# Turning two half chunks at once, and value preparation in slots of its own

## The chip, the cores and the metric

The kernel runs on one core of a Trainium2 chip. Its engines work side by side, each through its own list of instructions in order: TensorE (PE, matmuls and transposes; PEld is its loading of stationary operands), VectorE (DVE), ScalarE (ACT), GpSimd (POOL) and SyncE (SP), which here issues the DMAs. The metric is the device time of one execution in microseconds; lower is better. Before the change the median of three runs was 1085.4 us (1083.91 to 1087.75).

## What is computed

An attention over keys and values that are averaged in groups of 8 along the sequence, followed by a gated product of matrices without an activation:

```python
B, H, S, D = 8, 8, 576, 64          # batches, heads, sequence, head size
k_p = k.reshape(B, H, 72, 8, D).mean(axis=3)
v_p = v.reshape(B, H, 72, 8, D).mean(axis=3)
scores = (q @ k_p.T) / sqrt(D)      # per batch and head, 576 x 72
attn = softmax(scores)
o = attn @ v_p                      # 576 x 64 per head
x = o over all heads, 4608 tokens x 512
out = ((x @ w_a) * (x @ w_b)) @ w_out     # w_a, w_b 512 x 1536, w_out 1536 x 512
```

All data are float32. The kernel keeps near float32 precision with matmuls in fp32r: each operand is split into a high part and a low part (`low_part`, L188, subtracts the high part from the source), and three products (high x high, high x low, low x high) are summed.

## The kernel before

**The long part.** The 4608 tokens are cut into 9 tiles of 512 (t = 0 to 8). For each tile and each of 12 slices f of the 1536 hidden columns, `ffn_in` makes 24 matmuls of 512 columns (12 into psa, L635 to L637, then 12 into psb), `gated` multiplies the two on DVE (h, L592), `split_gated` splits the product into hh and hl, and `ffn_out` adds 12 matmuls into four accumulators (L657 to L659). After a tile's last slice the accumulators are copied to y and stored through SP (L666). This is 36 matmuls per slice and tile, 3888 in all, and the order of these items is written out by hand in `order`.

**The attention in between.** The attention of a later tile is worked out between the matmuls of the tile before. Tokens are taken in chunks of 128 or 64 (`chunks_of`): a batch of 576 tokens is four chunks of 128 and one of 64, the 64 last in even batches and first in odd ones. From tile 2 on, the two neighbouring halves of 64 (the last of an even batch and the first of the next) form one *band* that goes through scores and softmax together, the first half in partitions 0 to 63 and the second in 64 to 127. There are three such bands, in tiles 3, 5 and 7.

`chunk` loads a band's queries, splits them (qh, ql), makes the scores on PE (psc, L452 and L459), sums their halves on DVE (s, L466), subtracts the maximum (L419, L420), takes the exponential on ACT (L480) and the sum and its inverse on DVE (L482 to L484), scales on POOL (L486), and splits the probabilities into pr (high and low, for 64 of the 72 pooled keys) and rem (the other 8). Then each unit of the band (one chunk of 128, or each of the two halves of 64) is handed to `turn_unit`: for x = 0, 1 four transposes each, for x = 2 two transposes (L538) into a PSUM tile ptr, followed by one ACT copy (L539) into the block's operand `turned[j][x]`. A *block* is one to three units of one batch within one tile. When its last unit is turned, the block's value products follow: matmuls po (L573 to L576) against vdiag and vrem, whose result becomes xh and xl, the input of `ffn_in`.

psc, ptr and po share one ring of two PSUM buffers with the tag "att". An instruction that writes such a buffer waits until the reader of the buffer's former content is done.

**Keys and values.** `load_values(b)` loads a batch's values in three pairs of DMAs into a ring of two buffers ("kv", shared with the keys), reduces each of the six over its groups of 8 on DVE (vp, L339), writes the high part to vdiag on ACT (L344), spreads the remainder into the temporary vwide (two instructions, L348), copies it to vrem on ACT (L359), writes vdiag's low part in two instructions on DVE (L362), and finally vrem's low part (L188). vdiag and vrem exist twice, by b % 2. vwide is from the ring "tmp" of six places, which queries, stored outputs y and others use as well.

**What sets the order.** Every engine runs its instructions in the order in which the program writes them. `Chains` decides that order: each of these pieces of work is a generator. `chains.step()` is called twice per psa or psb group and twice per `ffn_out`, that is once for each six matmuls; one call is a *slot*. `yield n` puts a generator off by n slots, `yield PE` lines it up for work on PE, of which one is let through per slot. Within a slot, generators run by rank: products, splits, chunks, weights, keys and values. The work between two yields goes to the engines without a break. `plan` starts each band's `chunk` some slots ahead of its need, `load_keys` of the next batch 18 slots (`KEYS_AHEAD`) ahead of that, and `load_values` 16 slots (`VALUES_AFTER`) behind the keys, so two slots ahead of the chunk. The slot arithmetic knows no engine's time: an instruction that is late simply delays what is written behind it on its engine.

Batches 0 and 1 are prepared at the start, beside the conversion of the weights; batch 2 falls at the end of that phase, and batches 3 to 7 into the long part.

Of the kernel before, what the change touches and what calls it, by code (L numbers as in the profile page):

```python
# [10 lines left out]
F32R = mybir.dt.float32r  # L11
# [9 lines left out]
P = 128  # L21
# [5 lines left out]
NK = DM // P  # L27
# [20 lines left out]
NG = H // 4  # L48
# [4 lines left out]
BLOCK, BLOCK_LATER = 256, 384  # L53
# [26 lines left out]
class Chains:  # L80
# [9 lines left out]
    def mark(self, *what):  # L90
        self.done.add(what)
# [30 lines left out]
def attn_moe_kernel(ctx: ExitStack, tc: tile.TileContext, q, k, v, vr, wa, wb, wo, out):  # L122
    nc = tc.nc
    const = ctx.enter_context(tc.tile_pool(name="const", bufs=1))
    sb = ctx.enter_context(tc.tile_pool(name="sb", bufs=2))
# [12 lines left out]
    ident = const.tile([P, P], F32R, name="ident")  # L138
# [16 lines left out]
    bands, i = [], 0  # L155
# [157 lines left out]
    def load_values(b):  # L313
        vd = vdiag[b % 2]
        vrem = sb.tile([P, NG, 2, 2, D], F32R, tag="vrem", name=f"vrem_{b}")
        yield from wait(("keys", b, 2), ("values", b - 1))
        vp = sb.tile([P, NK + NG, D], F32, tag="vp", name=f"vp_{b}", bufs=1)
        for x0 in range(0, NK + NG, 2):
            if b == 0:
                vraw = [early_v[:, x, :] if x < NK else early_vr[:, x - NK, :] for x in (x0, x0 + 1)]  # L320
            else:
                if x0:
                    yield from wait(("vraw", b, x0 - 2))
                vraw = [sb.tile([P, S], F32, tag="kv", name=f"vraw_{b}_{x0 + j}")[:, :D * POOL] for j in range(2)]
                for j in range(2):
                    if x0 < NK:
                        nc.sync.dma_start(vraw[j], v[b, :, x0 + j, :])
                    else:
                        nc.sync.dma_start(vraw[j][:NR], vr[b, :, x0 + j - NK, :])
                yield 3  # L330
            for j in range(2):
                x, rows = x0 + j, P if x0 < NK else NR
                vv = vraw[j][:rows].rearrange("p (d j) -> p d j", j=POOL)
                if b == 0 and 0 < x < NK:
                    for n in (4, 2, 1):
                        to = vp[:rows, x].unsqueeze(2) if n == 1 else vv[:, :, :n]
                        nc.gpsimd.tensor_tensor(out=to, in0=vv[:, :, :n], in1=vv[:, :, n:2 * n], op=ALU.add)
                else:
                    nc.vector.tensor_reduce(out=vp[:rows, x], in_=vv, axis=AX.X, op=ALU.add)  # L339
            mark("vraw", b, x0)  # L340
            yield 1
        for e in range(2):
            r = slice(e * KM, e * KM + KM)
            nc.scalar.mul(vd[r, :, 0, r], vp[r, :NK], 1.0 / POOL)  # L344

        wide = tmp(f"vwide_{b}").rearrange("p (r j e d) -> p r (j e) d", r=NG, j=2, e=2)
        for r in range(NG):
            nc.vector.scalar_tensor_tensor(  # L348
                out=wide[:NR, r],
                in0=vp[:NR, NK + r].unsqueeze(1).broadcast_to([NR, 4, D]),  # L350
                scalar=1.0 / POOL,
                in1=mask[:NR].unsqueeze(2).broadcast_to([NR, 4, D]),
                op0=ALU.mult,
                op1=ALU.mult,
            )
        wide = wide.rearrange("p r c d -> p (r c d)")
        vrf = vrem.rearrange("p r j e d -> p (r j e d)")
        yield 1
        nc.scalar.copy(vrf[:NR], wide[:NR])  # L359
        for e in range(2):  # L360
            r = slice(e * KM, e * KM + KM)
            nc.vector.scalar_tensor_tensor(  # L362
                out=vd[r, :, 1, r],
                in0=vp[r, :NK],
                scalar=1.0 / POOL,
                in1=vd[r, :, 0, r].bitcast(F32),
                op0=ALU.mult,
                op1=ALU.subtract,
            )
        yield 1  # L370
        r = slice(2 * 4 * KR, NR)
        low_part(nc.vector, vrf[r], wide[r], vrf[r])
        yield 1
        vrems[b] = vrem
        mark("values", b)

    def chunk(i):
# [121 lines left out]
        low_part(nc.gpsimd, pr[:n, 1], s[:n, :, :KM], pr[:n, 0])  # L499
        low_part(nc.gpsimd, rem[:n, :, 1], sr, rem[:n, :, 0])  # L500
        mark("probs", i)
        for u, us in units:
            yield 1 if soon else PROBS_GAP
            yield from turn_unit(u, pr[us], rem[us], ident[us, us])
        mark("turned", i)

    def turn_unit(i, pr, rem, ident):

        b, o, n = flat[i]
        t, col = divmod(b * S + o, NT)  # L510
        soon = t < 2
        j = block_of[i]
        members = blocks[j]
        c0 = sum(flat[c][2] for c in members if c < i)
        total = sum(flat[c][2] for c in members)
        if i == members[0]:
            turned[j] = {}

        def turn(x):
            rows = P if x < 2 else NR  # L520
            num = NK if x < 2 else NG
            if x not in turned[j]:
                if tile_of[i] < 2:
                    turned[j][x] = sb.tile([P, num, BLOCK], F32R, tag=f"p{x}", name=f"p{x}_{j}", bufs=1)
                elif x == 0:
                    both = sb.tile([P, 2, NK, BLOCK_LATER], F32R, tag="work", name=f"p_{j}", bufs=1)
                    turned[j].update({0: both[:, 0], 1: both[:, 1]})
                else:
                    turned[j][x] = sb.tile([P, NK * BLOCK], F32R, tag="p0", name=f"p{x}_{j}", bufs=1)[
                        :, :NG * BLOCK_LATER  # L530
                    ].rearrange("p (g s) -> p g s", g=NG)
            dst = turned[j][x]
            pt = ps.tile([P, 512], F32, tag="att", name=f"ptr_{i}_{x}", bufs=2)
            ptr = pt.bitcast(F32R).rearrange("p (g s) -> p g s", g=NK)
            for g in range(num):
                src = pr[:, x, 2 * g:2 * g + 2, :] if x < 2 else rem[:, g]
                src = src.rearrange("p a s -> p (a s)") if x < 2 else src.rearrange("p a c s -> p (a c s)")
                nc.tensor.transpose(ptr[:rows, g, :n], src, ident)  # L538
            nc.scalar.copy(dst[:rows, :, c0:c0 + n], ptr[:rows, :num, :n])  # L539

        yield from wait(("turn", i - 1), ("value", j - 1))
        if t >= 2:
            yield from wait(*(("weight", name, NF - 1) for name in ("a", "b", "o")))
        for x in range(3):
            if x < 2 or t < 2:
                yield PE
            turn(x)
            if x != 1 or t < 2:
                yield 1
        mark("turn", i)  # L550
        if i != members[-1]:
            return
        yield 1 if soon else VALUE_GAP
        yield from wait(("values", b))
        if t not in xtiles:
            xtiles[t] = [sb.tile([P, NK, NT], F32R, tag=x, name=f"{x}_{t}") for x in ("xh", "xl")]
        xh, xl = xtiles[t]
        vd, vrem = vdiag[b % 2], vrems[b]
        cols = slice(col + n - total, col + n)
        per = min(NK, 512 // total)  # L560
        th, tl, tr = (turned[j][x] for x in range(3))
        for g0 in range(0, NK, per):
            yield PE
            if j == 0:
                po = ps.tile([P, 512], F32, tag="psb" if g0 else "psa", name=f"po_{j}_{g0}")
            else:
                po = ps.tile([P, 512], F32, tag="att", name=f"po_{j}_{g0}", bufs=2)
            pov = po[:, :per * total].rearrange("p (g s) -> p g s", g=per)
            for g in range(g0, g0 + per):
                if per == NK and g == NK // 2:  # L570
                    yield PE
                dst = pov[:, g - g0, :]
                nc.tensor.matmul(dst, vd[:, g, 0, :], th[:, g, :total], start=True, stop=False)  # L573
                nc.tensor.matmul(dst, vd[:, g, 0, :], tl[:, g, :total], start=False, stop=False)
                nc.tensor.matmul(dst, vd[:, g, 1, :], th[:, g, :total], start=False, stop=False)  # L575
                nc.tensor.matmul(  # L576
                    dst,
                    vrem[:NR, g // 2, g % 2].rearrange("p e d -> p (e d)"),
                    tr[:NR, g // 2, :total],
                    start=False,  # L580
                    stop=True,
                )
            gs = slice(g0, g0 + per)
            nc.scalar.copy(xh[:, gs, cols], pov)
            yield 1
            low_part(nc.vector, xl[:, gs, cols], pov, xh[:, gs, cols])
        mark("value", j)
        del turned[j]
# [231 lines left out]
```

## Time and profile before

| | us |
|---|---|
| median of three runs | 1085.4 |
| the profiled execution, its own time | 1088.85 |
| its span, first to last instruction | 1087.1 |
| PE busy | 1035.4 (95%) |
| DVE busy | 566.6 (52%) |
| ACT busy | 510.6 (47%) |
| POOL busy | 503.3 (46%) |

The mean granted clock of PE over the span was 0.987 of full speed. A row of the timeline gives start, length (both in us), engine, line, operation, result and operands with their size, how many were merged, and in brackets how long the engine stood idle before it and who released it. A row of a stretch gives its bounds and length, the busy us of PE, PEld, DVE, ACT and POOL with counts of instructions, the granted clock of PE, the share of time that DMA engines were busy, and GB/s. A row of groups gives busy us, the mean ns of one, and the idle time before them.

### The profile page before, as it was taken

Reading aid. Unit: us, or ns where it says so; the run is one execution under the profiler, and the core shown is the slowest. Engines: PE = TensorE matmul, PEld = TensorE weight load, DVE = VectorE, ACT = ScalarE, POOL = GpSimd, SP = SyncE. Lnnn points to the kernel's source line nnn. Section 1 sums busy time; section 2 is a strip of 40 time slices with the busy share of each in tenths; the row PEclk is TensorE's granted clock in tenths of the full one; section 3 lists DMA queues with packets and bytes.
Section 4 is the critical chain, followed back from the end, with each engine's and each line's share of the span. In section 5 each row is a group of like instructions: output and inputs, shape, how many; then the busy total and the mean of one; then the engine's idle time right before and its main releaser. Section 6 shows DMA issues by size and latency. Waiting matters only on the chain.

```text
span 1087.1 us, 13530 instructions
## 1 busy us (share of the span) xinstructions
PE 1035.4 (95%) x4964; PEld 860.9 (79%) x4964; DVE 566.6 (52%) x914; ACT 510.6 (47%) x1023; POOL 503.3 (46%) x428
## 2 busy tenths in 40 slices
PE   4568999999999999999999999999999999999998
PEld 4456788788878888888878888888878888888886
DVE  7889967744672346544672337543573344322112
ACT  3656645445554445444544445444544354443332
POOL 6322200045474555555554555554554355555442
PEclk9979999999999999999999999999999999999999
DMA  6335445214220003000320003100310010001001
GB/s 219 105 120 155 147 136 170 92 54 137 77 96 1 1 23 126 27 1 1 100 85 1 1 1 109 44 1 1 121 54 2 1 59 1 1 1 39 1 1 39
DMA packets 32178, 63.79 MB, mean 59 GB/s; under 512 B 7376, under 2 KB 7376, under 8 KB 32112
## 3 DMA queue, kind: packets, MB, share of 16 engines
q1 hardware_dynamic: 32112, 62.93, 18.0%
q8 instruction: 39, 0.64, 0.2%
q14 instruction: 27, 0.22, 0.1%
HBM read 51.38 MB, written 11.53 MB: 58 GB/s over the span
## 4 chain that ended last, share of the span: by engine, by line
PE 84%; DVE 10%; ACT 3%; DMA 2%; issue 1%; POOL 0%; SPq 0%; DVEq 0%; ACTq 0%; POOLq 0%
PE psb L635 9%; PE acc L657 9%; PE psb L637 8%; PE psb L636 8%; PE psa L635 8%; PE acc L659 8%; PE acc L658 8%; PE psa L636 8%; PE psa L637 8%; PE ptr L538 2%; PE psc L452 2%; DVE vp L339 1%; DVE vwide L348 1%; PE po L575 1%; PE psc L459 1%
## 5 line engine op out<-in xcount | busy, mean ns | idle before, releaser
L592 DVE TENSOR_TENSOR h<-psb,h 128x512 f32<-128x512 f32 x108 | 74.6, 691 | 352.6 <-PE psb L637 345.5
L188 POOL TENSOR_TENSOR jlb<-wb_raw,jhb 128x512 fp32r<-128x512 f32 x88 | 115.1, 1308 | 271.4 <-ACT jhb L267 271.4
L188 POOL TENSOR_TENSOR jlo<-wo_raw,jho 128x512 fp32r<-128x512 f32 x108 | 142.9, 1323 | 116.8 <-ACT jho L267 116.8
L642 ACT COPY h<-psa 128x512 f32<-128x512 f32 x108 | 63.5, 588 | 242.3 <-PE psa L637 230.9
L635 PE MATMUL psb<-xh,jhb 128*128 128x512 f32 x432 | 173.3, 401 | 0.8 <-DVE h L592 0.8
L635 PE MATMUL psa<-xh,jha 128*128 128x512 f32 x432 | 173.2, 401 | 0.0
L657 PE MATMUL acc<-jho,hh 128*128 128x512 f32 x432 | 171.9, 398 | 0.0
L636 PE MATMUL psa<-xl,jha 128*128 128x512 f32 x432 | 169.5, 392 | 0.7 <-DVE xl L188 0.7
L637 PE MATMUL psb<-xh,jlb 128*128 128x512 f32 x432 | 169.8, 393 | 0.0
L636 PE MATMUL psb<-xl,jhb 128*128 128x512 f32 x432 | 169.7, 393 | 0.0
L637 PE MATMUL psa<-xh,jla 128*128 128x512 f32 x432 | 169.6, 393 | 0.0
L659 PE MATMUL acc<-jho,hl 128*128 128x512 f32 x432 | 168.6, 390 | 0.0
L658 PE MATMUL acc<-jlo,hh 128*128 128x512 f32 x432 | 168.3, 389 | 0.0
L188 POOL TENSOR_TENSOR jla<-wa_raw,jha 128x512 fp32r<-128x512 f32 x88 | 121.8, 1384 | 78.7 <-ACT jha L267 71.6
L605 ACT CAST hh<-h 128x512 fp32r<-128x512 f32 x100 | 62.2, 622 | 93.6 <-DVE h L592 89.6
L188 DVE TENSOR_TENSOR hl<-h,hh 128x512 fp32r<-128x512 f32 x100 | 85.5, 855 | 35.8 <-ACT hh L605 35.6
L637 PEld LDWEIGHTS psb<-xh,jlb 128*128 128x128 f32 x432 | 81.9, 190 | 17.6
L637 PEld LDWEIGHTS psa<-xh,jla 128*128 128x128 f32 x432 | 81.8, 189 | 17.5
L635 PEld LDWEIGHTS psb<-xh,jhb 128*128 128x128 f32 x432 | 82.1, 190 | 16.7 <-DVE h L592 1.2
L659 PEld LDWEIGHTS acc<-jho,hl 128*128 128x128 f32 x432 | 81.1, 188 | 17.5
L636 PEld LDWEIGHTS psa<-xl,jha 128*128 128x128 f32 x432 | 82.0, 190 | 15.8 <-DVE xl L188 1.1
L636 PEld LDWEIGHTS psb<-xl,jhb 128*128 128x128 f32 x432 | 82.2, 190 | 15.1
(95 smaller groups left out, 1678.2 us busy)
## 6 DMA issues: line engine op xcount, KB each, us to landing
out<-y SPq DMA_DIRECT2D x36, 256.0 KB, 2.1
kraw<-in_k SPq DMA_DIRECT2D x28, 288.0 KB, 3.3
qraw<-in_q SPq DMA_DIRECT2D x28, 256.0 KB, 3.6
vraw<-in_v SPq DMA_DIRECT2D x28, 256.0 KB, 2.9
words<-in_wa SPq DMA_DIRECT2D x12, 512.0 KB, 3.5
words<-in_wb SPq DMA_DIRECT2D x12, 512.0 KB, 3.5
words<-in_wo SPq DMA_DIRECT2D x12, 512.0 KB, 3.5
vraw<-in_vr SPq DMA_DIRECT2D x14, 192.0 KB, 2.8
```

The lines of the kernel that those rows point to most:

```text
L188: eng.tensor_tensor(out=lo, in0=src, in1=hi.bitcast(F32), op=ALU.subtract)
L452: nc.tensor.matmul(pt[:n, :2 * hk], qh[:, g, :n], kd[:, g].rearrange("p w e s -> p (w e s)"), start=(x == 0), stop=False,)
L538: nc.tensor.transpose(ptr[:rows, g, :n], src, ident)
L592: nc.vector.tensor_tensor(out=h, in0=pt, in1=h, op=ALU.mult)
L605: nc.scalar.copy(hh, h)
L635: nc.tensor.matmul(pt, wh[:, c], xh[:, kk], start=(kk == 0), stop=False)
L636: nc.tensor.matmul(pt, wh[:, c], xl[:, kk], start=False, stop=False)
L637: nc.tensor.matmul(pt, wl[:, c], xh[:, kk], start=False, stop=(kk == NK - 1))
L642: nc.scalar.copy(h, pt)
L657: nc.tensor.matmul(acc[c], hh[:, cs], wh, start=first, stop=False)
L658: nc.tensor.matmul(acc[c], hh[:, cs], wl, start=False, stop=False)
L659: nc.tensor.matmul(acc[c], hl[:, cs], wh, start=False, stop=last)
```

## The change

Two things are changed. In `load_values`, for batches 2 to 7, a yield is put behind each reduction, behind each vwide instruction, and two slots behind each low-part instruction of vdiag; batches 0 and 1 stay as they were. In `turn_unit`, the first half of a two-half band transposes all 128 rows at once; the first 64 columns of the result go to its own block's operand as before, and the other 64 are copied by ACT to a tile kept aside (in buffers p1 and p2, which the first two tiles used). When the second half's turn comes, it takes no PE work, and ACT copies the kept columns to its block's operand.

```diff
@@ load_values
                 else:
                     nc.vector.tensor_reduce(out=vp[:rows, x], in_=vv, axis=AX.X, op=ALU.add)
+                if b > 1:
+                    yield 1
             mark("vraw", b, x0)
             yield 1
...
             nc.vector.scalar_tensor_tensor(out=wide[:NR, r], ...)
+            if b > 1:
+                yield 1
...
             nc.vector.scalar_tensor_tensor(out=vd[r, :, 1, r], ...)
+            if b > 1:
+                yield 2
         yield 1
@@ chunk
+        halves = {}
         for u, us in units:
             yield 1 if soon else PROBS_GAP
-            yield from turn_unit(u, pr[us], rem[us], ident[us, us])
+            yield from turn_unit(u, pr[:n], rem[:n], halves, us.start > 0)
@@ turn_unit
-    def turn_unit(i, pr, rem, ident):
+    def turn_unit(i, pr, rem, halves, kept):
...
-        soon = t < 2
+        soon, full = t < 2, pr.shape[0]
...
             dst = turned[j][x]
+            if kept:
+                nc.scalar.copy(dst[:rows, :, c0:c0 + n], halves[x][:rows])
+                return
             pt = ps.tile([P, 512], F32, tag="att", name=f"ptr_{i}_{x}", bufs=2)
...
-                nc.tensor.transpose(ptr[:rows, g, :n], src, ident)
+                nc.tensor.transpose(ptr[:rows, g, :full], src, ident[:full, :full])
             nc.scalar.copy(dst[:rows, :, c0:c0 + n], ptr[:rows, :num, :n])
+            if n < full:
+                if x != 1:
+                    tag, shape = ("p2", [P, NG, BLOCK]) if x else ("p1", [P, NK, BLOCK])
+                    half = sb.tile(shape, F32R, tag=tag, name=f"half{x}_{i}", bufs=1).rearrange("p g s -> p (g s)")
+                    for y in (x,) if x else (0, 1):
+                        halves[y] = half[:, y % 2 * NK * n:][:, :(NG if y == 2 else NK) * (full - n)].rearrange(
+                            "p (g s) -> p g s", s=full - n
+                        )
+                nc.scalar.copy(halves[x][:rows], ptr[:rows, :num, n:full])
...
         for x in range(3):
-            if x < 2 or t < 2:
+            if (x < 2 or t < 2) and not kept:
                 yield PE
             turn(x)
```

## The prediction

> **What bounds the kernel now.** I read the page's first lines, then the busy time by stretches, then the rows of TensorE (PE) that began late, then what VectorE (DVE) was doing just before them.
>
> ```profile
> span 1087.1 us, 13530 instructions
> PE 1035.4 (95%) x4964; PEld 860.9 (79%) x4964; DVE 566.6 (52%) x914; ACT 510.6 (47%) x1023; POOL 503.3 (46%) x428
> ```
>
> ```profile
> 316.00:557.00 241.00, 241.00 (x1177) 201.32 (x1176) 120.86 (x190) 114.75 (x234) 130.34 (x108) 1.00 0.13 41
> 557.00:564.20 7.20, 4.79 (x18) 3.92 (x17) 6.46 (x10) 1.96 (x4) 2.44 (x3) 0.76 0.06 23
> 564.20:813.40 249.20, 249.20 (x1220) 208.43 (x1218) 121.29 (x192) 118.06 (x240) 132.44 (x110) 1.00 0.11 36
> 813.40:820.50 7.10, 4.69 (x21) 3.83 (x19) 6.09 (x10) 1.46 (x3) 1.92 (x3) 0.76 0.00 0
> ```
>
> In the stretches (length, then busy us of PE, PEld, DVE, ACT, POOL, then the granted clock) PE is busy for all of 241.0 and 249.2 us at clock 1.00. There only two things shorten the kernel: less work on PE, or the removal of the few places where PE stands. From 193 us on, PE's late rows are these five:
>
> ```profile
> 199.31 0.50 PE L635 MATMUL psb<-xh,jhb 128*128 128x512 f32 x1 [0.76 <-DVE h L592]
> 211.31 0.40 PE L452 MATMUL psc<-kdiag,qh 128*128 128x288 f32 x1 [1.69 <-DVE s L466]
> 312.88 0.40 PE L452 MATMUL psc<-kdiag,qh 128*128 128x288 f32 x1 [1.18 <-DVE s L466]
> 560.26 0.54 PE L452 MATMUL psc<-kdiag,qh 128*128 128x288 f32 x1 [2.40 <-DVE s L466]
> 816.14 0.43 PE L452 MATMUL psc<-kdiag,qh 128*128 128x288 f32 x1 [2.41 <-DVE s L466]
> ```
>
> Together 8.44 us. Four are score matmuls (L452) that need a buffer of the ring "att", which the score sum on DVE (L466) empties late. DVE was late because the value preparation stood in front of it:
>
> ```profile
> 207.91 1.28 DVE L339 TENSOR_REDUCE vp<-vraw 96x64 f32<-96x512 f32 x2 [2.58 <-DMA vraw<-in_vr]
> 310.55 1.78 DVE L188 TENSOR_TENSOR vrem<-vwide,vrem 32x512 fp32r<-32x512 f32 x1
> 435.24 0.75 DVE L348 SCALAR_TENSOR_TENSOR vwide<-vp,mask 96x256 f32<-96x256 f32 x2
> 553.83 1.23 DVE L339 TENSOR_REDUCE vp<-vraw 96x64 f32<-96x512 f32 x2
> 556.01 1.85 DVE L348 SCALAR_TENSOR_TENSOR vwide<-vp,mask 96x256 f32<-96x256 f32 x2
> 557.78 1.94 DVE L362 SCALAR_TENSOR_TENSOR vdiag<-vp,vdiag 64x256 fp32r<-64x256 f32 x2
> 559.75 0.82 DVE L466 TENSOR_REDUCE s<-psc 128x144 f32<-128x288 f32 x2
> ```
>
> Batch 5: two pairs, 1.85 and 1.94 us, run in one piece ahead of the sum at 559.75. Each stretched pair is two short instructions (batch 4's vwide pair took 0.75 us), the second of which ends with a POOL instruction beside it:
>
> ```profile
> 556.27 1.30 POOL L188 TENSOR_TENSOR pr<-s,pr 128x512 fp32r<-128x512 f32 x1 [0.73 <-ACT pr L495]
> ```
>
> Behind three of the five stalls the clock sinks:
>
> ```profile
> 211.30:215.60 4.30, 4.29 (x13) 3.48 (x14) 2.84 (x7) 0.46 (x2) 0.00 (x0) 0.61 0.00 0
> 560.20:564.20 4.00, 3.94 (x14) 3.54 (x15) 3.33 (x7) 0.00 (x0) 0.00 (x0) 0.57 0.00 0
> 816.10:820.50 4.40, 4.36 (x19) 3.83 (x19) 3.46 (x6) 0.00 (x0) 0.00 (x0) 0.61 0.00 0
> ```
>
> Work at clock c loses (1 - c) of its time: 0.39 x 4.30 + 0.43 x 4.00 + 0.39 x 4.40 = 5.1 us.
>
> **The change, first part: values in slots of their own.** A slot is six 512-column matmuls, 6 x 0.23 = 1.4 us where nothing else is put in (the spacing is quoted below). Counting yields from a batch's first reduction: before, the reductions (L339) stand at slots 0, 0, 4, 4, 8, 8, vwide at 9, 9, vdiag at 10, 10, the vrem low part at 11. After, for batches 2 to 7: reductions 0, 1, 6, 7, 12, 13, vwide 15, 16, vdiag 18 and 20, vrem 23, done at 24. The chunk planned with the same begin reaches its score sums at slots 9 to 11 (its load waits 5, its two query steps 1 and QUERY_GAP 4); in batch 3, whose chunk waits for another, at 12 and 13. So in batches 2, 4, 5, 6 and 7 nothing of the values stands at slots 9 to 11, and in batch 3 one reduction per slot (0.6 us, half of the 1.23 us pair) stands where vwide, vdiag and vrem stood before. I count the four score stalls as gone: 1.69 + 1.18 + 2.40 + 2.41 = 7.7 us. The stall at 199.31 has two reductions ahead of h (L592); one moves behind it: 0.6 of the 0.76 us. With the clock's 5.1 us: 13.4 us.
>
> [...] By the rows, each of the three stalls from 1.69 us up has its dip and no dip lies within the two long full stretches; I go by the rows.
>
> Where the moved work lands, DVE has room:
>
> ```profile
> 564.20:582.00 17.80, 17.80 (x90) 14.32 (x89) 4.46 (x8) 8.77 (x20) 10.57 (x9) 1.00 0.00 1
> ```
>
> After batch 5's old place DVE is busy 4.46 of 17.8 us. The five pieces add at most 1.85 + 1.94 + 1.78 = 5.6 us there. Without this cover they would be back in front of the sums, at the old price.
>
> What the stretch makes late is the value product. Batch 7 has the least room:
>
> ```profile
> 792.41 1.27 DVE L339 TENSOR_REDUCE vp<-vraw 128x64 f32<-128x512 f32 x2
> 816.48 0.68 DVE L188 TENSOR_TENSOR vrem<-vwide,vrem 32x512 fp32r<-32x512 f32 x1
> ```
>
> ```profile
> 857.04 0.19 PE L573 MATMUL po<-p,vdiag 128*128 128x64 f32 x1
> ```
>
> Eleven slots took 24.1 us, 2.2 each with everything put in; 12 more are 26 us against 857.04 - 817.16 = 39.9 us of room, so 13 us are left, less two slots by which the second half gets earlier: no cost.
>
> The moved steps issue DMAs: second and third pair of value loads leave 2 and 4 slots later on SP's queue. In batch 4 the second pair thereby falls behind the stores of a finished tile:
>
> ```profile
> 425.36 3.02 SPq L666 DMA_DIRECT2D out<-y  x4
> vraw<-in_v SPq DMA_DIRECT2D x28, 256.0 KB, 2.9
> ```
>
> At worst 3.0 + 2.9 us to landing against three slots (4.2 us): DVE would wait 1.7 us, with an h (L592) behind it that PE needs only some slots later. I take 0 and keep 1.7 for the range. In batch 2 it goes the other way: five slots instead of four lie between the second pair's last reduction and the use of the third, so the 2.58 us wait for the load should shrink; it is in the stall at 211.31 already. The temporary vwide is held from slot 15 to 23 instead of 9 to 11; its ring has six places and fewer than six requests fall in that time: 0.
>
> **Second part: one turn for two halves.** Three bands (tiles 3, 5, 7) hold two halves of 64. What a turn costs PE is the start of the second matmul behind it less the last start ahead of it, less two matmuls:
>
> ```profile
> 423.25 0.39 PE L637 MATMUL psb<-xh,jlb 128*128 128x512 f32 x1
> ...
> 424.08 0.39 PE L658 MATMUL acc<-jlo,hh 128*128 128x512 f32 x1
> ...
> 425.01 0.39 PE L659 MATMUL acc<-jho,hl 128*128 128x512 f32 x1
> ...
> 425.98 0.39 PE L658 MATMUL acc<-jlo,hh 128*128 128x512 f32 x1
> ```
>
> ```profile
> 574.30 0.39 PE L636 MATMUL psb<-xl,jhb 128*128 128x512 f32 x1
> 574.53 0.39 PE L637 MATMUL psb<-xh,jlb 128*128 128x512 f32 x1
> ...
> 575.62 0.39 PE L658 MATMUL acc<-jlo,hh 128*128 128x512 f32 x1
> ...
> 576.52 0.39 PE L659 MATMUL acc<-jho,hl 128*128 128x512 f32 x1
> ...
> 577.75 0.40 PE L658 MATMUL acc<-jlo,hh 128*128 128x512 f32 x1
> ```
>
> Spacing 0.23 us, so a whole chunk of ten transposes costs 0.83 + 0.97 - 4 x 0.23 = 0.88 us and a half of ten 1.09 + 1.23 - 0.92 = 1.40 us: a half is dearer than a whole. A band goes from 2.80 to 0.88 us; 3 x 1.92 = 5.8 us.
>
> It adds three copies on ACT per band:
>
> ```profile
> L539 ACT CAST p<-ptr 128x256 fp32r<-128x256 f32 x16 | 5.9, 372 | 16.1 <-PE ptr L538 16.0
> L539 ACT CAST p<-ptr 96x128 fp32r<-96x128 f32 x8 | 2.1, 265 | 0.0
> ```
>
> 2 x 0.37 + 0.27 = 1.0 us, 3.0 in all, on an engine busy 8.8 of 17.8 us in the stretch above. The first buffer of "att" is held 0.37 us longer, but its next user comes about 2 us after it (the two groups start at 574.5 and 576.5). Without that room: 3.0 us. The copies of the second half no longer wait for PE. I take 0.
>
> **Sum.** 13.4 + 5.8 = 19.2 us: span 1087.1 - 19.2 = 1067.9. The profiled execution took 1088.85, so 1069.7 by its own time. That execution is 3.45 us above the median of the three shown (1085.4): from the median 1066.2. Clock dips are what I would expect to differ between executions, and then the median had less to lose; I take the middle, 1068.0, with 1064 to 1072 as its own range.
>
> **Rivals.**
> - The stalls return in part. For: the pieces still meet POOL one by one, and batch 3 still has a reduction in each slot of its sums. Against: batch 4 carried all pieces beside its sums without a PE wait. Half of 13.4 lost: 1074.7.
> [...]
> - The values part does not do what it says, because POOL's hold, not the order, makes DVE late: 1068.0 + 13.4 = 1081.4. Against: the held pieces no longer stand before a sum.
> - Slower. Five pieces spread over 24 slots each meet a POOL instruction, and in a longer stretch some chunk's sums always stand behind a held one. Price 2.40 + 1.72 = 4.1 us per stall; it decides from 19.2 / 4.1 = 4.7 new stalls, and one per batch (six) gives 1068.0 + 24.6 = 1092.6. For: the rows with 1.85, 1.94 and 1.78 us. Against: a single piece leaves most of a slot free, and slots 9 to 11 are empty of values. [...]
>
> **Chances.** Forecast 0.62, stalls in part 0.16, dips stay 0.08, values part idle 0.08, slower 0.06. About 0.3% (3.3 us) is what a measurement here tells from no change. Of the values-part case I give 0.03 to faster, 0.05 to no change: faster 0.89, same 0.05, slower 0.06. The range 1062 to 1077 holds the first three.
>
> **What would show it.** Right: no PE row waiting for L466 behind 193 us; vwide, vdiag and vrem one by one between other DVE work; clock 1.00 through the former dips; 30 fewer transposes, none in the form 64x128 in tiles 3, 5, 7; nine more ACT copies. Wrong: a PE wait for DVE at 12 or more slots behind a batch's first reduction, PE waiting for ACT's p in the three bands, or a value product held by vrem in batch 7.

## The result

The changed kernel takes 1068.96 us (median of four runs, 1068.24 to 1069.69) against 1084.89 us of the kernel before in the same comparison. The ratio is 0.9849, 95% interval 0.9828 to 0.987: 15.9 us faster. Forecast: 1068.0 us, range 1062 to 1077. Repeated beside other runs it was 1069.58 against 1086.36, ratio 0.9843 (0.983 to 0.9857).

The first lines of the profile after, whose execution took 1068.24 us:

```profile
span 1066.5 us, 13486 instructions
PE 1023.5 (96%) x4934; PEld 854.5 (80%) x4934; DVE 575.4 (54%) x914; ACT 511.8 (48%) x1032; POOL 504.3 (47%) x428
```

PE has 30 instructions less, ACT nine more, as listed in the prediction. PE's rows that began late behind 193 us are now two instead of five:

```profile
197.08 0.50 PE L655 MATMUL psb<-xh,jhb 128*128 128x512 f32 x1 [0.17 <-DVE h L612]
306.83 0.40 PE L458 MATMUL psc<-kdiag,qh 128*128 128x288 f32 x1 [1.01 <-DVE s L472]
```

The sum of the waits fell from 8.44 to 1.18 us. The stretches (bounds and length; then busy us of PE, PEld, DVE, ACT, POOL; then the granted clock) show 744 us without a gap where before there were two gaps and two dips of the clock:

```profile
193.00:217.00 24.00, 23.83 (x109) 19.56 (x108) 19.34 (x34) 9.92 (x21) 4.01 (x4) 1.00 0.21 70
300.00:316.00 16.00, 14.99 (x80) 12.41 (x79) 12.13 (x23) 8.56 (x18) 8.85 (x8) 1.00 0.52 176
316.00:1060.00 744.00, 744.00 (x3598) 623.76 (x3597) 337.65 (x509) 338.22 (x682) 395.49 (x323) 1.00 0.09 29
```

DVE around batch 5 after the change. The two pairs of score sums (L472) come first, with nothing of the values right ahead of the second; vwide, vdiag and vrem follow:

```profile
547.87 0.94 DVE L472 TENSOR_REDUCE s<-psc 128x144 f32<-128x288 f32 x2 [0.29 <-PE psc L465]
550.24 0.94 DVE L472 TENSOR_REDUCE s<-psc 128x144 f32<-128x288 f32 x2 [1.42 <-PE psc L465]
...
552.68 0.67 DVE L339 TENSOR_REDUCE vp<-vraw 96x64 f32<-96x512 f32 x1
...
556.94 2.81 DVE L350 SCALAR_TENSOR_TENSOR vwide<-vp,mask 96x256 f32<-96x256 f32 x2
559.67 1.51 DVE L366 SCALAR_TENSOR_TENSOR vdiag<-vp,vdiag 64x256 fp32r<-64x256 f32 x1
...
563.40 1.03 DVE L366 SCALAR_TENSOR_TENSOR vdiag<-vp,vdiag 64x256 fp32r<-64x256 f32 x1
...
565.18 0.68 DVE L188 TENSOR_TENSOR vrem<-vwide,vrem 32x512 fp32r<-32x512 f32 x1
```

The pieces are no shorter: vwide takes 2.81 us where it took 1.85. Nor did the yields part them all: vwide's two instructions and the first of vdiag run back to back, from 556.94 to 561.18. They are merely where nobody on PE waits. And DVE now waits for PE ahead of the second pair of sums (1.42 us), where before PE waited for DVE.

The one turn of a two-half band in tile 5, PE in order of time:

```profile
562.18 0.39 PE L657 MATMUL psb<-xh,jlb 128*128 128x512 f32 x1
562.41 0.45 PE L549 MATMUL ptr<-ident,pr 128*128 128x128 f32 x4
562.70 0.46 PE L677 MATMUL acc<-jho,hh 128*128 128x512 f32 x1
563.00 0.40 PE L678 MATMUL acc<-jlo,hh 128*128 128x512 f32 x1
...
563.92 0.39 PE L679 MATMUL acc<-jho,hl 128*128 128x512 f32 x1
...
564.89 0.40 PE L678 MATMUL acc<-jlo,hh 128*128 128x512 f32 x1
```

By the prediction's rule it costs 0.82 + 0.97 - 0.92 = 0.87 us (forecast 0.88) where two turns cost 2.80.

### The profile page after: what moved, and what is told of

Its sections match the earlier page's. It is cut to its first block, busy times and chain, and to the rows that moved or that the text cites. A ratio compares the mean times of both kernels' runs of the same rounds, so it can differ in the third digit from the quotient of the medians.

```text
span 1066.5 us, 13486 instructions
## 1 busy us (share of the span) xinstructions
PE 1023.5 (96%) x4934; PEld 854.5 (80%) x4934; DVE 575.4 (54%) x914; ACT 511.8 (48%) x1032; POOL 504.3 (47%) x428
## 4 chain that ended last, share of the span: by engine, by line
PE 86%; DVE 7%; ACT 3%; DMA 2%; issue 1%; POOL 0%; SPq 0%; DVEq 0%; ACTq 0%; POOLq 0%
PE acc L677 9%; PE psb L655 9%; PE acc L679 9%; PE acc L678 9%; PE psa L655 9%; PE psb L657 9%; PE psb L656 9%; PE psa L656 9%; PE psa L657 9%; PE ptr L549 2%; PE psc L458 2%; DMA wo_raw<-in_vr 1%; PE psc L465 1%; PE po L595 1%; PE po L596 1%
## 5 line engine op out<-in xcount | busy, mean ns | idle before, releaser
L655 PEld LDWEIGHTS psa<-xh,jha 128*128 128x128 f32 x432 | 81.6, 189 | 14.9
```

Of the source, the lines that this page charges most:

```text
L655: nc.tensor.matmul(pt, wh[:, c], xh[:, kk], start=(kk == 0), stop=False)
```

## The experiments

**1. Each part alone.** The diffs are the two halves of the change: one kernel leaves out the three yields, the other leaves `turn_unit` and its call as they were.

> One turn for two halves, the values prepared as before. If the two parts add up as in the sum: 5.8 us below the kernel before, about 1079.1 us, with the five PE waits for DVE and the three clock dips still there. If the first part needs the second (the saved PE time is lost again in the same stalls): within 2 us of before. If the whole gain is the turn: near 1069.

Measured: 1078.86 us (1076.3 to 1080.55) against 1086.1, ratio 0.9931 (0.991 to 0.9953), 7.2 us faster (forecast 1079.1). The stalls stood where they were:

```profile
210.69 0.40 PE L452 MATMUL psc<-kdiag,qh 128*128 128x288 f32 x1 [1.68 <-DVE s L466]
310.67 0.40 PE L452 MATMUL psc<-kdiag,qh 128*128 128x288 f32 x1 [1.18 <-DVE s L466]
556.09 0.40 PE L452 MATMUL psc<-kdiag,qh 128*128 128x288 f32 x1 [2.40 <-DVE s L466]
809.86 0.40 PE L452 MATMUL psc<-kdiag,qh 128*128 128x288 f32 x1 [2.40 <-DVE s L466]
```

Behind the first of them the clock did not fall this time (1.00 from 210.6 to 215.0 us, where it was 0.61 before). That missing dip, about 1.7 us (0.39 of 4.30 us), may be why the turn alone gained more than its 5.8.

> Values in slots of their own, each half turned by itself. By the sum: 13.4 us below the kernel before, about 1071.5 us, PE waits for L466 behind 193 us down from 7.7 us to about 1, clock 1.00 behind them, 60 transposes of halves (six halves of ten) still there. If POOL's hold and not the order makes the sums late: the stalls stay, within 3 us of before. If the clock dips are not the stalls' doing: about 1076.6, with the dips left at full clock loss of 5.1 us.

Measured: 1074.8 us (1074.43 to 1075.56), ratio 0.9898 (0.988 to 0.9916), 11.3 us faster. The waits, summed (us, times, longest), from 130 us on:

```profile
PE psc L458 <- DVE s L472: 0.8, 1, 0.8
PE psb L641 <- DVE h L598: 0.2, 1, 0.2
```

The time lies between two forecasts, 1071.5 if the dips go with the stalls and 1076.6 if they stay; the profile decides, with clock 1.00 in all of 130 to 1060 us (0.995 over the whole execution). What follows: both parts gain, and nothing shows that one needs the other; 7.2 + 11.3 = 18.5 us against 15.9 to 16.8 for both together, which their intervals allow. The stalls went with the yields and not with the turn. The order on DVE did it: the "does not do what it says" rival falls.

**2. Is a half dear because it is narrow?** From the changed kernel, each half takes a turn of its own at full width, and ACT takes the half's columns out:

```diff
-            if kept:
-                nc.scalar.copy(dst[:rows, :, c0:c0 + n], halves[x][:rows])
-                return
...
-            nc.scalar.copy(dst[:rows, :, c0:c0 + n], ptr[:rows, :num, :n])
+            nc.scalar.copy(dst[:rows, :, c0:c0 + n], ptr[:rows, :num, us])
...
-            if (x < 2 or t < 2) and not kept:
+            if x < 2 or t < 2:
```

> As changed, but the two halves are turned each in its own turn, both at the full width of 128 rows, and nothing is kept aside: 20 full transposes per band instead of 10. If a half is dear because it is 64 wide (1.40 us against 0.88 for a whole): 3 x 0.88 = 2.6 us above the changed kernel, about 1071.6 us. If a turn costs the same whatever its width: 3 x 1.4 = 4.2 us above, about 1073.2. If the second turn is free beside other work: no change, 1069.

Measured: 1072.45 us (1071.89 to 1072.67), ratio 0.9873 (0.9859 to 0.9888). The changed kernel stood at 1068.96 and 1069.58 in other comparisons, so 2.9 to 3.5 us above it: near the 2.6 of the first theory, though the 4.2 of the second (1073.2 us) is only 0.75 us off. The neighbour in the same comparison separates them better: the kernel with two narrow turns per band (1074.8) is 2.35 us slower, with ranges that do not meet. So twenty wide transposes cost less than twenty narrow ones; 3 x (2.80 - 1.76) = 3.1 us was the forecast of that difference. The rows settle it. The second half's own wide turn in tile 5, where a narrow one cost 1.40 us:

```profile
584.27 0.39 PE L644 MATMUL psb<-xh,jlb 128*128 128x512 f32 x1
...
585.10 0.39 PE L665 MATMUL acc<-jlo,hh 128*128 128x512 f32 x1
...
586.03 0.39 PE L666 MATMUL acc<-jho,hl 128*128 128x512 f32 x1
...
587.00 0.39 PE L665 MATMUL acc<-jlo,hh 128*128 128x512 f32 x1
```

That is 0.83 + 0.97 - 0.92 = 0.88 us, the price of a whole chunk.

**3. Place or spacing?** The change both moves the value work and pulls it apart. First moved without spacing: the old packed order, with one yield of six slots ahead of vwide.

```diff
-                if b > 1:
-                    yield 1
             mark("vraw", b, x0)
             yield 1
+        if b > 1:
+            yield 6
...
-            if b > 1:
-                yield 1
...
-            if b > 1:
-                yield 2
```

> As changed, but the values are prepared without the new yields (packed as before: reductions at slots 0,0,4,4,8,8), with one yield of 6 slots ahead of vwide, which puts vwide at 15,15, vdiag at 16,16 and vrem at 17. If the place in DVE's order is what counts: no PE wait for a score sum above 0.5 us in batches 5 and 7, clock 1.00, within 2 us of the changed kernel (about 1069). If the spacing counts: the packed pairs (1.85 and 1.94 us) still make PE wait, now for another DVE result, 2 to 4 us per batch, about 1076 to 1083.

Measured: 1068.86 us (1068.52 to 1069.27), ratio 0.9841 (0.9827 to 0.9856): the same as the changed kernel. No score matmul waits at all. DVE at batch 7, and PE beside it in the stretches:

```profile
806.95 2.81 DVE L350 SCALAR_TENSOR_TENSOR vwide<-vp,mask 96x256 f32<-96x256 f32 x2
809.68 1.98 DVE L364 SCALAR_TENSOR_TENSOR vdiag<-vp,vdiag 64x256 fp32r<-64x256 f32 x2
811.58 1.78 DVE L188 TENSOR_TENSOR vrem<-vwide,vrem 32x512 fp32r<-32x512 f32 x1
```

```profile
806.90:813.40 6.50, 6.50 (x33) 5.39 (x32) 6.44 (x7) 3.98 (x10) 6.38 (x6) 1.00 0.00 1
```

6.4 us of value work without a break, stretched as before, and PE is busy for all of the 6.5 us. Slots "of their own" are not needed; being away from the sums is enough.

Then spacing with hardly any move: single pieces in the very slots of the sums, though the second piece of vdiag and vrem thereby go from slots 10 and 11 to 12 and 13:

```diff
-                if b > 1:
-                    yield 1
             mark("vraw", b, x0)
...
-        yield 1
+        if b < 2:
+            yield 1
         nc.scalar.copy(vrf[:NR], wide[:NR])
...
             if b > 1:
-                yield 2
-        yield 1
+                yield 1
+        if b < 2:
+            yield 1
```

> One turn for two halves as changed; the reductions packed as before (0,0,4,4,8,8), then one piece per slot with no gap: vwide at 9 and 10, vdiag at 11 and 12, vrem at 13, so that single pieces stand in the very slots of the score sums. If spacing alone cures the stalls: no PE wait for a sum above 0.5 us in batches 5 and 7, about 1069 us. If place alone does: each sum still has a piece of up to 1.5 us ahead of it, PE waits of 0.5 to 1.5 us in most batches, mostly too short for a clock dip, about 1072 to 1075.

Measured: 1069.71 us (1068.7 to 1072.05), ratio 0.9857 (0.9834 to 0.9879). Waits from 130 us on, and the longest and batch 5's of them:

```profile
PE psc L458 <- DVE s L472: 2.2, 3, 1.3
```

```profile
210.61 0.40 PE L458 MATMUL psc<-kdiag,qh 128*128 128x288 f32 x1 [1.35 <-DVE s L472]
552.61 0.40 PE L458 MATMUL psc<-kdiag,qh 128*128 128x288 f32 x1 [0.42 <-DVE s L472]
```

Here my theory of the place failed in half: it expected waits in most batches and 1072 us at least. In this profile 5.5 of the 7.7 us of waits are gone. The pieces did not all come apart, though. Ahead of batch 5's first sum, at 552.11, DVE shows vwide's pair in one piece:

```profile
550.33 1.85 DVE L348 SCALAR_TENSOR_TENSOR vwide<-vp,mask 96x256 f32<-96x256 f32 x2
```

vdiag, 1.94 us in front of that sum before, now stands behind it. The 1.35 us in batch 2 come after DVE has waited 2.68 us for a load (before: 2.58). Neither the full move nor full spacing is needed; what counts, by these two runs, is how much DVE work stands between a score matmul and its sum. Experiment 5 puts a number on that.

**4. Do the slots say where a wait will be?** The packed kernel, moved by 3 slots instead of 6 (`yield 3`), so that only batch 3's sums meet the values.

> As the packed and moved kernel, but moved by 3 slots instead of 6: vwide 12,12, vdiag 13,13, vrem 14. The slots of the sums are 9 to 11 in batches 2, 4, 5, 6 and 7 and 12 and 13 in batch 3. If the slots decide: a PE wait for a score sum of 1 to 3 us in batch 3 alone (near 310 us), none in the others; about 1070 to 1073. If any heavy DVE stretch makes PE wait: waits in batches 5 and 7 as well, 1075 or more.

Measured: 1068.27 us in a single run. Behind 200 us there is one late row, in batch 3:

```profile
309.35 0.51 PE L545 MATMUL ptr<-ident,pr 128*128 128x128 f32 x4 [0.73 <-DVE s L468]
```

The place is as forecast, and the only one. The size is not (0.73 against 1 to 3 us), and the one that waits is a transpose that needs the second sum's buffer, not a score matmul.

**5. How much fits ahead of a sum, and do waits pull the clock down?** From the changed kernel, 3 to 8 extra reductions ahead of each chunk's first score sum from tile 4 on; their result is overwritten.

```diff
+                if g == 0 and t > 3:
+                    for _ in range(3 + i % 6):
+                        nc.vector.tensor_reduce(
+                            out=z[:n], in_=raw["a"][:n, 0, :].rearrange("p (d j) -> p d j", j=D), axis=AX.X, op=ALU.add
+                        )
```

> As changed, with 3 to 8 idle reductions on DVE (about 0.6 us each, result overwritten) ahead of the first score sum of every chunk from tile 4 on, so that PE waits a graded time, about 0.6 us less the 1.2 us of slack per count: 0.6 to 3.7 us. If PE's standing still makes the clock sink: the dips come behind the longer waits only, at full length (a loss of about 1.7 us each), and none behind waits below about 1.5 us. If the dips are not the waits' doing: no relation, or none at all. Time about 1069 + 20 waits of 2 us on average + half of them with a dip: 1110 to 1130 us.

Measured: 1135.66 us in a single run, above the range that I gave. 110 reductions made 18 waits of 40.9 us in all. The mean duration of one, the sum of the waits, and six of the 18 rows:

```profile
L474 DVE TENSOR_REDUCE z<-wa_raw 128x8 f32<-128x512 f32 x110 | 75.2, 684 | 3.1
```

```profile
PE psc L458 <- DVE s L477: 40.9, 18, 4.5
```

```profile
494.55 0.40 PE L458 MATMUL psc<-kdiag,qh 128*128 128x288 f32 x1 [1.49 <-DVE s L477]
526.01 0.61 PE L458 MATMUL psc<-kdiag,qh 128*128 128x288 f32 x1 [2.68 <-DVE s L477]
680.85 0.40 PE L458 MATMUL psc<-kdiag,qh 128*128 128x288 f32 x1 [2.09 <-DVE s L477]
709.90 0.42 PE L458 MATMUL psc<-kdiag,qh 128*128 128x288 f32 x1 [2.22 <-DVE s L477]
745.74 0.40 PE L458 MATMUL psc<-kdiag,qh 128*128 128x288 f32 x1 [3.20 <-DVE s L477]
777.13 0.61 PE L458 MATMUL psc<-kdiag,qh 128*128 128x288 f32 x1 [4.11 <-DVE s L477]
```

The granted clock in the 4 to 5 us behind five of them (the number ahead of the last two):

```profile
494.50:499.00 4.50, 4.45 (x21) 3.71 (x22) 2.70 (x5) 2.09 (x4) 0.23 (x1) 1.00 0.00 0
680.80:685.00 4.20, 4.15 (x19) 3.47 (x20) 3.93 (x7) 1.42 (x3) 0.00 (x0) 1.00 0.21 66
745.70:750.00 4.30, 4.26 (x20) 3.58 (x21) 3.21 (x6) 0.69 (x1) 0.54 (x1) 1.00 0.00 0
709.90:714.00 4.10, 4.10 (x13) 3.36 (x14) 3.33 (x6) 0.31 (x1) 0.00 (x0) 0.58 0.01 4
777.10:781.40 4.30, 4.27 (x12) 3.60 (x13) 2.76 (x5) 0.40 (x1) 0.00 (x0) 0.50 0.00 0
```

Five extra reductions made waits of 1.49, 2.09 and 1.73 us, eight made 4.47, 3.22, 4.11 and 3.45: on average 1.77 and 3.81, so 0.68 us each, and the line meets zero at 2.4 reductions. The other counts lie near it: three made 0.86, 0.72 and twice no wait, four 0.53 to 0.82, seven 2.94 to 3.20. So, as an estimate from this run, about 1.6 us of further DVE work (2.4 x 0.68) can stand ahead of a sum before PE notices (1.2 were expected). That fits experiment 3 (behind vwide's 1.85 us PE waited 0.42) and the kernel before (vwide and vdiag, 1.85 + 1.94 = 3.8 us: 3.8 - 1.6 = 2.2 us, where 2.40 were waited).

All 18 waits, sorted by the spacing of the 512-column matmuls behind them: none of the six up to 1.49 us (0.53, 0.58, 0.72, 0.82, 0.86, 1.49) was followed by a stretch at 0.42 to 0.43 us per matmul instead of 0.23; ten of the twelve from 1.73 to 4.47 us were, and two (2.09 and 3.20) were not. So in this run the waits did pull the clock down, from 1.73 us on and not every time. In the 8 us behind each of the ten the granted clock was 0.61 to 0.80, a loss of 20 us in all, 2.0 each. With the waits that makes 61 of the 66 us by which this kernel is slower than the changed one; the other 5 us are not traced.

**6. The wait that is left.** In batch 3 of the changed kernel DVE waits for the third load, which SP could issue only behind stores of y. DVE, then SP's queue:

```profile
305.73 0.68 DVE L339 TENSOR_REDUCE vp<-vraw 96x64 f32<-96x512 f32 x1 [1.87 <-DMA vraw<-in_vr]
306.33 0.81 DVE L472 TENSOR_REDUCE s<-psc 128x144 f32<-128x288 f32 x2
```

```profile
299.45 3.12 SPq L686 DMA_DIRECT2D out<-y  x2
302.67 0.85 SPq L329 DMA_DIRECT2D vraw<-in_vr  x2
```

The experiment writes the second and third pair of loads down two slots earlier, and leaves every instruction in its slot:

```diff
-                yield 3
+                yield 5 if b > 1 and x0 else 3
...
-                if b > 1:
+                if b > 1 and j == 0:
                     yield 1
             mark("vraw", b, x0)
-            yield 1
+            if b < 2:
+                yield 1
+            elif x0 == NK:
+                yield 2
```

> The changed kernel once more, as the measure for the run beside it: about 1069 us, with one PE wait for a score sum of about 1.0 us in batch 3.

> As changed, with every instruction of the values in the same slot, but the loads of a batch's second and third pair are written down two slots earlier, right behind the reductions that free their buffers. If the wait of 1.01 us that the changed kernel has left in batch 3 comes from the third load standing behind the stores of y on SP's queue: DVE's wait for in_vr there (1.87 us) and PE's wait are gone, about 1.2 us faster than the changed kernel. If the single reduction in the slot of the sums makes the wait: it stays, same time.

Measured: 1068.94 us (1068.56 to 1069.59) against 1069.58 (1068.45 to 1070.37) of the changed kernel beside it. The changed kernel's wait in batch 3 was 0.45 us this time, with 1.3 us of DVE waiting for in_vr; here both are gone, and the loads stand ahead of the stores:

```profile
297.14 4.49 SPq L329 DMA_DIRECT2D vraw<-in_vr  x2
301.91 4.77 SPq L689 DMA_DIRECT2D out<-y  x4
```

The mechanism is shown in these rows; the 0.64 us in the time (1.2 were forecast) is not told apart from nothing. No version here is told apart from the changed kernel as faster.

## Why the prediction was right, point by point

- **The bound.** PE's gaps and PE's own work were the right place to look. Between the two profiles the span fell by 20.6 us. Of that, 1.65 us lie ahead of the change: the last wait of the start, for xl, ended at 129.11 us before and at 127.46 after. The other 18.95 us stand against a sum of 19.2. That is closer than the medians allow: see "Which base".
- **The four score stalls, 7.7 us.** Gone, all but 1.01 us in batch 3, where I had said that one short reduction in the slot would not matter. The reduction did not; its load, which falls behind stores of y, did (experiment 6). A wait for DVE at slot 12 or later is also one of the signs that I had named for being wrong. In batch 4 the same thing came as forecast: DVE waited 2.38 us (at worst 1.7 in the prediction) for the second pair, and PE did not wait. So the SP step was right where I looked, and I did not look at batch 3.

```profile
424.58 0.69 DVE L339 TENSOR_REDUCE vp<-vraw 128x64 f32<-128x512 f32 x1 [2.38 <-DMA vraw<-in_v]
```

- **The stall for h, 0.6 of 0.76 us.** In the first profile 0.17 us were left, as forecast; in the profile of the repeat 0.86. Over all kernels, this wait was 0.76 or 0.77 us in the five profiles with packed reductions, and with spread ones 0.17 in three and 0.82 to 1.10 in three. So it did not respond reliably to the change.
- **The clock, 5.1 us.** That the waits bring the dips held (experiment 5: behind ten of the twelve waits from 1.73 us on), the size did not repeat: the kernel with the turn alone had waits of 1.68, 2.40 and 2.40 us, and the first had no dip behind it (1.00; 0.67 in the 5.0 and 5.2 us that begin with the other two), while the kernel before had one (0.61) behind 1.69 us. Why one wait brings a dip and another of about the same length does not, no run shows. The rival that the dips stay (1068.0 + 5.1 = 1073.1 us) is refuted: the changed profile has clock 1.00 in all stretches from 130 us on.
- **The turn, 5.8 us.** Right. One turn took 0.87 us by the rows. Between two kernels of the same comparison that differ in the turn, and in the values only by packed against spaced, lie 1074.8 - 1068.86 = 5.9 us. ACT's nine copies made no PE row wait from 130 us on.
- **Slots of their own.** The slot arithmetic named the right batches (experiment 4). The reason, that pieces must leave slots 9 to 11, was too strict: about 1.6 us of work may stay, by the estimate of experiment 5, which experiment 3 fits. And a slot in the program is no slot on DVE: the sign "one by one between other DVE work" was not met for vwide.
- **Which base, and some luck.** By medians the values part alone gained 11.3 us and not 13.4, and the whole 15.9 to 16.8 and not 19.2. The sum fits profile against profile, and those two are extremes: 1088.85 us is above every other run of the kernel before, 1068.24 the fastest of the changed kernel's four. So the sum was too large for a typical run, the clock's 5.1 us first of all, which come from one execution with three dips. The 1068.0 came within 1 us because the base was taken halfway between that execution and the median. The reason given, that dips differ between executions, stays open: the mean clock differed between executions of the kernel before (0.981 to 0.993 in nine), but also of the changed one (0.985 to 0.993 in four), and no run shows how much of it was dips. That half was the right share is luck. From the median alone, 1066.2, the forecast would have been 2.8 us off. The difference also shows in the spread: 4.2 us over the runs with the long stalls (1083.77 to 1087.96, and 1076.3 to 1080.55 with the turn alone), 1.1 and 0.75 us for the values alone and for packed and moved.
- **Slower by held pieces.** It did not happen, though its premise did: vwide grew from 1.85 to 2.81 us. That POOL's instructions make the pieces long was argued from rows standing side by side, and no run took POOL's work away, so that stays open.

## What to carry to other kernels

Where one engine is full, ask of every instruction queued on its helpers who stands behind it: in experiment 3 the same work cost nothing six slots later and 2.4 us of waiting right ahead of a result on which the full engine waits. Measure the slack with a graded dose of idle work; then order by hand only what exceeds it, and count the DMAs that move along. A long stall can cost a second time through the clock (in experiment 5 ten of the twelve waits from 1.73 us on did, 2.0 us each), so the longest gaps can be worth more than their length.

## What the runs showed of the hardware that I had not expected

- Ten transposes of 64 rows cost PE 1.40 us, ten of 128 rows 0.88 (experiment 2). In the profile of before the weight loads pause for 0.35 or 0.36 us ahead of each of the twelve narrow groups of four in tiles 3, 5 and 7 (4.3 us in all, 3.9 of them with no releaser that the profile shows); ahead of the 50 wide groups of four behind 130 us they stand 6.6 us in all, 0.13 each. One such row:

```profile
574.85 0.38 PEld L538 LDWEIGHTS ptr<-ident,pr 64*128 64x128 f32 x4 [0.35 <-issue]
```

- In experiment 5 the clock fell behind waits from 1.73 us on (ten of twelve; 0.50 and 0.58 in the two stretches shown, 0.42 to 0.43 us per matmul instead of 0.23), and behind none of the six up to 1.49 us. In between, 1.69 us had a dip behind it in the kernel before (0.61) and 1.68 us had none with the turn alone (1.00).
- A single vwide or vdiag instruction took up to 1.5 us (the vdiag at 559.67 above), where batch 4's pair of vwide took 0.75 us before the change.
